# One more group of four w2 tiles in seven products in the third block, with its rows loaded and scaled there, and the middle blocks' order written out anew

## The chip, the cores and the metric

The kernel runs on one core of a Trainium2 chip. The metric is the device time of one execution in microseconds (us). A time of a kernel is the median of several executions; the profile is one further execution, with its own span.

## The reference

Only the part that matters for the computation is shown; A is a state-space layer, B a dense layer with a mish activation, and both work on the same normalised rows.

```python
xn = _layernorm(x, axis=-1)                      # x: 2048 rows of 1024
# A: a complex diagonal state per column, scanned over the rows
Lam_bar = jnp.exp(dt * Lam)
B_bar = ((Lam_bar - 1.0) / Lam)[:, None] * Bmat
Bu = jnp.einsum("bld,pd->blp", xn + 0j, B_bar)
for t in range(L):
    h = Lam_bar[None, :] * h + Bu[:, t, :]
y = 2.0 * jnp.einsum("blp,dp->bld", hseq, Cmat).real + xn * Dskip
# B: 1024 -> 3584 -> 1024
g = jnp.einsum("bsd,df->bsf", xn, w1) + b1
sp = jnp.log1p(jnp.exp(-jnp.abs(g))) + jnp.where(g > 0, g, 0)
act = g * jnp.tanh(sp)
return x + y + jnp.einsum("bsf,fd->bsd", act, w2)
```

## The kernel before

The 2048 rows go through in four blocks of 512. A block normalises its rows, makes the hidden activations (product with w1, then mish), projects the rows into the state, scans, and at the end adds up in PSUM the product of the activations with w2 ("dense 2") and the output projection of the state. The first block (0 to 150 us) also prepares weights. In the second block the state projections are done in seven products instead of eight (sums of weight quarters against sums of row halves, Strassen's scheme), which costs VectorE, ScalarE and PSUM banks the work of putting the results together. The third and fourth block (`SPLIT`) also do the product with w1 that way, in seven "quads" of four tiles (letters p, q, s, w, x, y, z of `w_product` and `w_evacuate`; letters a to d are the state's `product` and `evacuate`), and most of dense 2.

**Dense 2 in the third block.** w2 has 28 tiles of 128 rows. A group g of four tiles (2g, 2g+1, 14+2g, 15+2g) can be done in seven products (`fast`, L1542) or as four plain tiles (`dense`, L1502). In the third block four groups go the fast way and twelve tiles plainly, in the fourth all seven groups:

```python
NFG = {2: 4, 3: GF}
PLAIN = [(f, f + 1) for f in (24, 10, 8, 22, 12, 26)]
PASSING = {8: 4, 22: 4}
```

The seven products run first (order `KIND`, L1209): of each product a TensorE matmul of 512 columns per tile pair and bank, then the plain tiles, eight matmuls a tile, then the state's projection. For a fast group its raw w2 rows are loaded (letter m, `d2_load`, on GpSimd's DMA queue), scaled row by row (letter h, `d2_row`, L1233, on ScalarE), and put into seven 256 KB units of a DRAM scratch `w2d`: three of them as they are, four as differences made by VectorE (`d2_sums`, L1252); each goes out as a GpSimd store (`d2_store`, L1230). A letter k in the order pops one pending sum with its store. The fifth group (tiles 8, 9, 22, 23) is plain in the third block, and its rows pass through the weight ring there as plain tiles; on that occasion ScalarE scales them into two free activation buffers (`PASSING`, `SCALED_AT`), and its sums and stores follow, so that the fourth block finds it in `w2d`.

**The ring.** All streamed weights go through seven slots of 512 KB (`ring`). SP issues the loads in a fixed order of items (`ring_load`, L426): "ws" (two 256 KB units of w1 quads, L455), "tp" (two units of `w2d`, L450), "w2" and "c" (a plain pair of tiles, a state row, L458). A load is issued when TensorE has finished with the slot's former item (`item_done`, L852), and it stands in SP's queue behind whatever was written there earlier. The stores of the second block's output (`O0`, L1692) go through SP as well.

**The order.** What stands around what is written by hand in two strings, `STEPS` for the third block and `LAST` for the fourth. Letters besides those above: r rotates a state column by its phase (`rotate_in`, L914 to L918 on VectorE: one operation of 2048 elements and two of 512), G scales an activation tile, g is mish, t makes the sums of activations for products 5, 6 and 7 (`act_sums`, L1363), u and I the first products of dense 2 and the evacuation of their banks ("kept", L1580), E the statistics of four 128-row tiles of the next block (`ln_stats_only`, L564 and L566), l loads the next block's x (four 256 KB loads on GpSimd, L398).

Of the kernel before, what the change touches and what calls it, by code (L numbers as in the profile page):

```python
# [9 lines left out]
P = 128  # L10
# [153 lines left out]
def build_kernel(nc, A_x, A_Lambda_re, A_Lambda_im, A_B_re, A_B_im, A_C_re, A_C_im,  # L164
# [43 lines left out]
    UNITS = [(REAL[QUADS.index(o[0])], int(o[1])) for o in STEPS.split() if o[0] in QUADS]  # L208
# [203 lines left out]
    items = []  # L412
    for blk in range(NB):
# [9 lines left out]
        items += [("c", j) for j in range(NJ)] if blk >= FAST else []  # L423
    n_loaded = [0]
# [573 lines left out]
    def w_product(blk, i, n):  # L998
# [28 lines left out]
        if not direct and half == len(units) - 1:  # L1027
            item_done()
# [160 lines left out]
    steps, later, held = [], [], []  # L1189
# [21 lines left out]
    D2_RAW += [(("a", 24), ("a", 10)), (("h", 0), ("h", 4)), (("h", 8), ("h", 12))]  # L1211
# [21 lines left out]
    def d2_row(n, slot=None):  # L1233
# [89 lines left out]
    CHUNKS = {2: ((0, 8),), 3: ((0, 6), (6, 12), (12, 14))}  # L1323
# [171 lines left out]
    def tail(blk, base):  # L1495
        near = blk < NB - 1
        first = [True] * 8

        def acc(u, lhsT, rhs, reads, last=False, tell=False, chained=False):
            st_ = first[u]  # L1500
            first[u] = False
            PE.mm(lambda e: e.matmul(ps[:, u, :], lhsT=lhsT, rhs=rhs, start=st_, stop=last, skip_group_check=blk in SPLIT),  # L1502
# [39 lines left out]
        def fast(n, i, k):  # L1542
# [9 lines left out]
            if n not in (1, 2, 3):  # L1552
                rhs = rhs.bitcast(f16)
# [486 lines left out]
```

## Time and profile before

| what | before |
|---|---|
| median of 3 runs | 587.75 us (587.65 to 588.03) |
| span of the profiled execution | 586.3 us |
| bytes moved by the DMA engines | 162.15 MB, mean 277 GB/s |

Stages of the third and fourth block, from the table of stretches (busy time of each engine; DMA is the mean busy share of the 16 DMA engines; the granted TensorE clock is 1.00 in every row):

| us | what runs | TensorE | VectorE | ScalarE | DMA | GB/s |
|---|---|---|---|---|---|---|
| 306.8 to 347.0 | block 3: quads p, q, s and state products a, b | 40.20 | 33.31 | 27.54 | 0.96 | 325 |
| 347.0 to 374.0 | products c, d, quads w to z | 26.95 | 24.35 | 22.29 | 0.99 | 349 |
| 374.0 to 391.5 | seven products of w2 and the last of quad z | 17.45 | 11.80 | 11.01 | 0.77 | 271 |
| 391.5 to 412.3 | twelve plain tiles | 20.70 | 20.59 | 18.57 | 0.86 | 245 |
| 412.3 to 446.9 | the state's projection, outputs | 34.44 | 34.19 | 6.89 | 0.64 | 221 |
| 446.9 to 487.0 | block 4: as the first row | 40.10 | 27.70 | 32.84 | 0.77 | 270 |
| 487.0 to 513.3 | as the second row | 26.29 | 21.64 | 23.12 | 0.89 | 319 |
| 513.3 to 586.3 | seven products of w2 for all groups, projection, outputs | 70.50 | 63.99 | 26.54 | 0.64 | 224 |

How to read it: a stage in which TensorE's busy time equals the length of the stretch is set by TensorE; where the DMA share is near 1 the DMA engines have nothing left. Busy time of matmuls is that of a pipeline, so the pace of one matmul is read from a group's busy time over its count. In the rows of the views, "out<-in" are the program's tile names, xN is a count, and "[0.52 <-ACT act L901]" behind an instruction is the idle time ahead of it on its engine and what ended it. In a table of waits the columns are time, count and longest; in the stretches, for each engine busy time and count, then granted clock, DMA share and GB/s.

### The profile page before, as it was taken

The page shows a single profiled execution, that of the slowest core. Times are in us where ns is not written, and L with a number is a line of the kernel's source. Part 1 is how long each engine was busy: PE and PEld are TensorE (multiplying, and loading weights), DVE is VectorE, ACT ScalarE, POOL GpSimd, SP SyncE. Part 2 cuts the span into 40 slices and gives each one's busy share as a digit, 9 for nine tenths or more (in the row PEclk, how much of TensorE's full clock was granted, in tenths as well). Part 3 has the DMA queues.
Part 4 walks back from the last instruction along what each step waited for, and adds up shares of the span by engine and source line. Part 5 has one row for each costly group of instructions (what it writes and reads, how often), then busy time and mean ns, then how long its engine had stood idle before and what let it go on. Part 6 is the DMA issues. An engine that isn't in the chain of part 4 may idle for free.

```text
span 586.3 us, 9768 instructions
## 1 busy us (share of the span) xinstructions
PE 581.0 (99%) x3599; PEld 353.9 (60%) x3635; DVE 513.4 (88%) x789; ACT 401.8 (69%) x541; POOL 150.7 (26%) x213
## 2 busy tenths in 40 slices
PE   9999999999999999999999999999999999999998
PEld 8644444444447887444448888644446888844444
DVE  6998999998997878999877889779999669789995
ACT  4859994658578868999916687959223798992330
POOL 2899300123524420441351241001010113100000
PEclk9999999999999999999999999999999999999999
DMA  9999998999688978999999899798865966998832
GB/s 244 306 243 247 245 186 202 316 301 360 185 303 287 357 249 293 316 321 255 345 375 345 305 309 382 257 344 209 306 210 191 346 237 241 326 324 318 293 113 73
DMA packets 116345, 162.15 MB, mean 277 GB/s; under 512 B 55882, under 2 KB 66762, under 8 KB 116298
## 3 DMA queue, kind: packets, MB, share of 16 engines
q1 hardware_dynamic: 99776, 109.67, 62.0%
q0 software_dynamic: 13440, 44.57, 21.7%
q10 hardware_dynamic: 3082, 7.29, 3.3%
q8 instruction: 29, 0.48, 0.3%
q14 instruction: 18, 0.15, 0.1%
HBM read 115.36 MB, written 34.08 MB: 255 GB/s over the span
## 4 chain that ended last, share of the span: by engine, by line
PE 93%; DVE 2%; ACT 2%; DMA 1%; issue 1%; POOL 0%; ACTq 0%; POOLq 0%
PE ps L1502 34%; PE ps L1024 19%; PE ps L948 13%; PE ps L1563 10%; PE ps L871 10%; PE ps L1438 5%; DMA act<-in_A_B_im_dram 1%; PE ps L680 1%; PE ps L689 1%; PE ps L642 1%; ACT act L894 1%; PE ps L1525 1%; ACT act L901 1%; DVE CT L835 0%; DVE CT L833 0%
## 5 line engine op out<-in xcount | busy, mean ns | idle before, releaser
L1502 PE MATMUL ps<-ring,act 128*128 128x512 bf16 x532 | 117.3, 379 | 0.6
L1502 PEld LDWEIGHTS ps<-ring,act 128*128 128x128 bf16 x544 | 53.2, 98 | 63.8
L1044 ACT ACTIVATE snaps<-ps,par,cs 128x256 f32<-128x256 f32 x100 | 54.4, 562 | 44.4 <-PE ps L1024 40.0
L1502 PE MATMUL ps<-ring,hT 128*128 128x512 bf16 x355 | 78.3, 379 | 0.4
L1024 PE MATMUL ps<-TT,ring 128*128 128x256 f16 x552 | 68.3, 273 | 0.0
L910 DVE TENSOR_TENSOR mt<-hT,tab 128x2048 bf16<-128x2048 bf16 (+1 forms) x56 | 67.9, 1213 | 0.4
L1502 PEld LDWEIGHTS ps<-ring,hT 128*128 128x128 bf16 x362 | 35.4, 98 | 42.7
L1453 DVE TENSOR_TENSOR_SCAN hT<-cs,qi,hT 128x512 bf16<-128x512 f32 x48 | 60.7, 1275 | 0.0
L1024 PEld LDWEIGHTS ps<-TT,ring 128*128 128x128 f16 (+1 forms) x552 | 53.8, 98 | 7.2 <-issue 0.2
L871 PE MATMUL ps<-xnT,ring 128*128 128x512 bf16 x258 | 56.8, 379 | 0.3
L1024 PE MATMUL ps<-xnT,ring 128*128 128x256 bf16 x424 | 53.9, 273 | 0.0
L1061 DVE SCALAR_TENSOR_TENSOR act<-ps,cs,snaps 128x512 bf16<-128x512 f32 x54 | 39.8, 748 | 15.2 <-PE ps L1024 13.3
L1024 PEld LDWEIGHTS ps<-xnT,ring 128*128 128x128 bf16 (+1 forms) x424 | 41.4, 98 | 5.4
L871 PEld LDWEIGHTS ps<-xnT,ring 128*128 128x128 bf16 x264 | 25.8, 98 | 30.9
L1230 POOL DMA_DIRECT2D w2d<-act x21 | 15.0, 718 | 110.5 <-ACT act L1240 54.9
L1473 ACT ACTIVATE hT<-hT,wz 128x1024 bf16<-128x1024 bf16 x16 | 18.1, 1146 | 34.3 <-DVE hT L1468 34.3
L1563 PE MATMUL ps<-ring,act 128*128 128x512 bf16 (+1 forms) x176 | 39.5, 379 | 0.2
L1230 POOL DMA_DIRECT2D w2d<-hb x28 | 20.0, 717 | 74.4 <-ACT hb L1240 33.0
L894 ACT ACTIVATE act<-act 128x2048 bf16<-128x2048 bf16 (+3 forms) x13 | 33.0, 2557 | 3.8 <-DVE act L1047 3.8
L973 DVE TENSOR_TENSOR hT<-ps,snaps 128x512 f16<-128x512 f32 x36 | 23.8, 687 | 12.3 <-ACT snaps L965 11.1
L1563 PEld LDWEIGHTS ps<-ring,act 128*128 128x128 bf16 (+1 forms) x180 | 17.6, 98 | 20.6
L1173 POOL DMA_DIRECT2D wsd<-hb x35 | 19.1, 548 | 39.0 <-DVE hb L1199 28.8
(240 smaller groups left out, 1085.2 us busy)
## 6 DMA issues: line engine op xcount, KB each, us to landing
ring<-wsd SPq DMA_DIRECT2D x122, 256.0 KB, 4.6
ring<-in_B_w_dram SPq DMA_DIRECT2D x54, 512.0 KB, 5.9
ring<-ctd SPq DMA_DIRECT2D x24, 512.0 KB, 4.4
ring<-w2d SPq DMA_DIRECT2D x24, 512.0 KB, 4.6
wsd<-hb POOLq DMA_DIRECT2D x35, 256.0 KB, 5.1
ring<-w2d SPq DMA_DIRECT2D x29, 256.0 KB, 3.8
w2d<-hb POOLq DMA_DIRECT2D x28, 256.0 KB, 5.5
w2d<-act POOLq DMA_DIRECT2D x21, 256.0 KB, 6.2
```

The lines of the kernel that those rows point to most:

```text
L871: PE.mm(lambda e, k=k, w=w: e.matmul(ps[:, bank, :], lhsT=w, rhs=xnT[:, k, :], start=k == 0, stop=k == NK - 1), reads=[b_ring[s]] + b_xnT, ...
L894: aop(lambda e: e.activation(t, t, AF.Mish), reads=b, writes=b)
L910: vop(lambda e: e.tensor_tensor(mt[:], u.unsqueeze(1).to_broadcast([P, 2, 2, TB]), tab[:, :, j, :].unsqueeze(2).to_broadcast([P, 2, 2, TB] ...
L948: PE.mm(lambda e, w=w, x=x, o=o, begin=begin, end=end: e.matmul(ps[:, bank, o:o + TH], lhsT=w, rhs=x, start=opens and begin, stop=end, ski ...
L1024: PE.mm(lambda e, w=w, x=x, o=o, begin=begin, end=end: e.matmul(ps[:, bank, o:o + TH], lhsT=w, rhs=x, start=opens and begin, stop=end, ski ...
L1044: aop(lambda e, o=o, p=p, j=j: e.activation(o, p, AF.Identity, scale=ig, bias=b1(f0 + j)), reads=[b_ps[b], b_par, b_ig], writes=b_dst)
L1061: vop(lambda e: e.scalar_tensor_tensor(out=dst, in0=bank(b), scalar=ig, in1=src, op0=ALU.mult, op1=ALU.add), reads=[b_ps[b], b_snap[k], b_ ...
L1230: PO.dma(lambda e: e.dma_start(w2d[at // 4][:, at % 4 * TB:(at % 4 + 2) * TB].rearrange("p (j t) -> p j t", j=2), t[:, :, d, :]), sem, rea ...
L1438: PE.mm(lambda e, j=j, ci=ci, k=k, bank=bank: e.matmul(ps[:, bank + ci, :], lhsT=BT[:, ci, j, k, :], rhs=xnT[:, k, :], start=k == 0, stop= ...
L1453: vop(lambda e: e.tensor_tensor_scan(out=hT[:, ci, j, :], data0=cj("r", j).to_broadcast([P, TB]), data1=hT[:, ci, j, :], initial=init, op0 ...
L1502: PE.mm(lambda e: e.matmul(ps[:, u, :], lhsT=lhsT, rhs=rhs, start=st_, stop=last, skip_group_check=blk in SPLIT), reads=reads, writes=[b_p ...
L1563: PE.mm(lambda e: e.matmul(ps[:, bank, :], lhsT=lhsT, rhs=rhs, start=st_, stop=end, skip_group_check=True), reads=b_t + [b_ring[s]], write ...
```

## The change

The fifth group of w2 is done in seven products in the third block too (`NFG[2]` 5, eight plain tiles instead of twelve). Its rows do not pass through the ring: they are loaded raw by GpSimd (m4) in the third block into activation buffers 8 and 12 and scaled there by VectorE (H16 to H19, `d2_row` with `queue=VE`), and sums and seven stores follow. Each sum over the activations covers ten tiles a half instead of eight.

The two strings are written anew: evacuations are operations of their own (e and the product's name), and what stood in the functions `tail`, `dense_part` and `dense_fast` (products D and X, kept banks kp, plain tiles pl, scans sc, outputs Y, Q, fin, ...) stands in the strings as well, run by a new function `split_block`. Rotations r3 to r7 stand between the seven products. The stores of the second block's output (now o0) stand between the quads x and z, and the next block's x is loaded (l0) behind z6 and g2 where it stood behind h7. A ring slot is freed when the last matmul that reads it is written, whichever product that is in.

```diff
-    NFG = {2: 4, 3: GF}
+    NFG = {2: 5, 3: GF}
-    PLAIN = [(f, f + 1) for f in (24, 10, 8, 22, 12, 26)]
-    PASSING = {8: 4, 22: 4}
-    SCALED_AT = {24: (8, 22), 10: (12,), 8: (26,)}
+    PLAIN = [(f, f + 1) for f in (24, 10, 12, 26)]
+    PASSING = {}
...
-             "b5 O0 a6 b6 O0 a3 h4 b3 S0 O0 a7 O0 h5 b7 k0 c2 d2 k0 h6 a4 b4 h7 l0 k0 c5 c1 k0 d5 d1 r0 c6 G0 c3 G1 d6 d3 c7 G2 w1 d7 r1 w5 w2 G3 c4 d4 k0 E0 E1 w6 x1 x5 x2 k0 w7 k0 w3 r2 "
-             "x6 w4 k0 y1 y5 y2 x7 x3 E2 E3 y6 x4 z1 z5 g2 z2 y7 y3 z6 G7 y4 g6 z3 z7 u0 t0 G8 u2 G9 z4 I2 G10 u1 t1 t2")
...
+             "es6 m1 q4 eq4 k0 k0 a2 ea2 g0 a1 ea1 s7 es7 b2 eb2 k0 s3 es3 b1 eb1 s4 es4 a5 ea5 b5 g1 eb5 k0 a6 ea6 h4 a3 O0 b6 ea3 m4 eb6 O0 S0 O0 a7 ea7 "
+             "b3 ed2 eb3 b7 O0 eb7 h5 c2 ec2 k0 a4 k0 h6 d2 h7 b4 ea4 G1 eb4 d5 ed5 k0 k0 c1 ec1 c5 r0 c6 ec5 d1 ed1 H16 H17 ec6 G0 c3 w1 ec3 d6 ed6 H18 "
+             "c7 ec7 d3 H19 ed3 G2 ew1 d7 ed7 w5 ew5 G3 c4 ec4 k0 w2 k0 d4 ew2 k0 r1 ed4 w6 ew6 x1 ex1 k0 G4 x5 ex5 w7 ew7 k0 x2 ex2 o0 w3 ew3 r2 x6 w4 k0 "
+             "ex6 y1 ey1 o0 y5 ew4 k0 ey5 y2 ey2 o0 x7 ex7 x3 ex3 y6 ey6 x4 o0 ex4 z1 ez1 z5 ez5 z2 ez2 y7 ey7 y3 z6 k0 g2 l0 ey3 ez6 G7 y4 ey4 g6 z3 ez3 "
+             "t0 z7 ez7 r3 D10 D11 G9 G11 G8 G10 z4 E0 ez4 kp2 D70 t1 G6 D71 G5 E1 g7 D20 G12 t2 D21 X5 E2 r4 kp0 E3 lr0 G13 r5 li0 r6 kp1 ns2 ns0 tr0 ns3 "
+             "r7 X6 tr3 kp3 pl24 tr2 pl10 ns1 tr1 pl12 sc00 sc01 sc10 pl26 to0 so0 sc11 T0 to1 X3 sc21 so1 al0 sc20 sc30 al1 to2 sc31 X4 so2 sc40 to3 al2 "
...
-    D2_RAW += [(("a", 24), ("a", 10)), (("h", 0), ("h", 4)), (("h", 8), ("h", 12))]
+    D2_RAW += [(("h", 8), ("h", 12)), (("h", 0), ("h", 4)), (("h", 8), ("h", 12))]
...
-    def d2_row(n, slot=None):
+    def d2_row(n, slot=None, queue=AC):
...
-        aop(lambda e: e.activation(o, x, AF.Copy, scale=wg[:, r:r + 1]),
-            reads=b_x + [b_wg], writes=b_t[2 * j:2 * j + 2])
+        put = ((lambda e: e.activation(o, x, AF.Copy, scale=wg[:, r:r + 1])) if queue is AC else
+               (lambda e: e.tensor_scalar(o, x, wg[:, r:r + 1], None, op0=ALU.mult)))
+        queue.op(put, reads=b_x + [b_wg], writes=b_t[2 * j:2 * j + 2])
...
-    CHUNKS = {2: ((0, 8),), 3: ((0, 6), (6, 12), (12, 14))}
+    CHUNKS = {2: ((0, 10),), 3: ((0, 6), (6, 12), (12, 14))}
...
+    def used(i):
+        left[i] -= 1
+        if left[i] == 0:
+            gone.add(i)
+            return True
+        return False
+
+    def release():
+        while n_item[0] in gone:
+            item_done()
...
+    def split_block(blk):
...
+        def mm2(bank, lhsT, rhs, reads, at, last=False, opens=False, chained=False, lo=0, hi=TB, tell=False):
+            freed = at is not None and used(at)
+            PE.mm(lambda e: e.matmul(ps[:, bank, lo:hi], lhsT=lhsT, rhs=rhs, start=opens, stop=last, skip_group_check=True),
+                  reads=reads, writes=[b_ps[bank]], first=opens or chained, last=last, chained=chained, tell=tell or freed)
+            if freed:
+                release()
...
+        run = {"r": rotate_in, "G": lambda n: act_scale(blk, n), "g": lambda n: mish(blk, n), "k": lambda n: pop_step(),
+               "m": d2_load, "M": lambda n: d2_load(n, AC), "h": d2_row, "H": lambda n: d2_row(n, queue=VE),
...
+               "E": lambda n: ln_stats_only(blk + 1, n), "S": lambda n: row_scales(), "l": lambda n: load_next(),
+               "K": lambda n: carry_on(), "O": lambda n: held.pop(0)(SP), "o": lambda n: held_out.pop(0)(SP),
```

GpSimd's queue where the third block prepares w2, before (`hb` and `act` are activation buffers, `xx` the rows of x, L1225 raw loads, L1230 stores to `w2d`, L1173 stores to the scratch of w1):

```order
L1225 DMA hb<-in_B_w_dram 128x2x1024 x2
L1173 DMA wsd<-hb 128x1024 x4
L1230 DMA w2d<-act 128x2x512 x2
L1230 DMA w2d<-hb 128x2x512 x3
L398 DMA xx<-in_A_x_dram 128x1024 x4
L1230 DMA w2d<-act 128x2x512 x2
L1230 DMA w2d<-hb 128x2x512 x4
L1230 DMA w2d<-act 128x2x512 x7
```

and now (L1263, L1268, L1211 and L407 are the same operations):

```order
L1263 DMA hb<-in_B_w_dram 128x2x1024 x2
L1211 DMA wsd<-hb 128x1024 x4
L1263 DMA hb<-in_B_w_dram 128x2x1024 x2
L1268 DMA w2d<-act 128x2x512 x2
L1268 DMA w2d<-hb 128x2x512 x3
L1268 DMA w2d<-act 128x2x512 x2
L1268 DMA w2d<-hb 128x2x512 x11
L407 DMA xx<-in_A_x_dram 128x1024 x4
```

A second raw load stands ahead of the stores, the fifth group's seven stores (the last seven of the x11, from `act` before) follow those of the fourth group directly, and the loads of x stand behind all of them.

SP's queue from the third block's first ring loads to the first loads for dense 2, before (L455 ring loads of w1 units, L450 of w2 units, L1692 output stores of 256 KB):

```order
L455 DMA ring<-wsd 128x1024 x32
L1692 DMA out_dram<-xx 128x1024
L455 DMA ring<-wsd 128x1024 x2
L1692 DMA out_dram<-xx 128x1024 x3
L1173 DMA wsd<-act 128x1024 x4
L455 DMA ring<-wsd 128x1024 x15
L450 DMA ring<-w2d 128x1024 x20
```

and now (L465, L460 and L1601 are the same operations):

```order
L1211 DMA wsd<-act 128x1024 x4
L465 DMA ring<-wsd 128x1024 x8
L1601 DMA out_dram<-xx 128x1024
L465 DMA ring<-wsd 128x1024 x4
L1601 DMA out_dram<-xx 128x1024
L465 DMA ring<-wsd 128x1024 x2
L1601 DMA out_dram<-xx 128x1024
L465 DMA ring<-wsd 128x1024
L460 DMA ring<-w2d 128x1024 x2
L1601 DMA out_dram<-xx 128x1024
L460 DMA ring<-w2d 128x1024 x23
```

The four output stores moved behind the stores to `wsd` and stand one by one among the last loads of w1 units and the first of w2 units.

VectorE in the seven products of w2, from the second sum over the activations on, before (L1363 the sums, L910 to L918 a rotation, L1580 the kept banks):

```order
L1363 TENSOR_TENSOR act<-act 128x8x256 x2
L910 TENSOR_TENSOR mt<-hT_49,tab 128x2048
L916 TENSOR_TENSOR hT<-mt 128x512
L918 TENSOR_TENSOR hT<-mt 128x512
L1580 SCALAR_TENSOR_TENSOR KS<-ps,wz,xx 128x512 x4
L910 TENSOR_TENSOR mt<-hT_49,tab 128x2048
```

and now, from the last sum on (L947 to L955 a rotation, L1702 kept banks, L574 and L576 the statistics of x, L614 and L615 the inverse root):

```order
L1402 TENSOR_TENSOR act<-act 128x10x256
L574 BN_STATS stats<-xx 128x6 x2
L576 BN_AGGR mv<-stats 128x2
L947 TENSOR_TENSOR mt<-hT_49,tab 128x2048
L953 TENSOR_TENSOR hT<-mt 128x512
L955 TENSOR_TENSOR hT<-mt 128x512
L1702 SCALAR_TENSOR_TENSOR KS<-ps,wz,xx 128x512 x2
L574 BN_STATS stats<-xx 128x6 x2
L576 BN_AGGR mv<-stats 128x2
L947 TENSOR_TENSOR mt<-hT_49,tab 128x2048
L953 TENSOR_TENSOR hT<-mt 128x512
L955 TENSOR_TENSOR hT<-mt 128x512
```

Statistics and rotations now stand between the sums and the kept banks, and the kept banks come in two pairs; the second pair follows after the inverse root and one more rotation.

More of the change, by code (lines that the diff above doesn't have):

```diff
@@ L1026, in w_product @@
                     reads=b_unit + b_x, writes=[b_ps[bank]], first=begin, last=end, chained=not opens)
[L1027 to L1028 removed]
+        if not direct and used(at):
+            release()
     def w_evacuate(blk, i, n, keep):
@@ L1542, in fast @@
-        def fast(n, i, k):
-            bank = BANKS[n][i]
-            st_ = first[bank]
-            first[bank] = False
-            p, ng = KIND.index(n), 2 * NFG[blk]
-            at = p * ng + k
-            if near and p >= 5:
-                at += 4 * len(PLAIN) + -5 * ng % 4
-            s = (base + at // 4) % NRING
-            rhs = ring[:, s, at % 4 * TB:(at % 4 + 1) * TB]
-            if n not in (1, 2, 3):
-                rhs = rhs.bitcast(f16)
-            if n in (1, 2, 4):
-                t, b_t = place(blk, k + (n != 1) * NF // 2)
-                q = i if n == 4 else 2 + i
-                lhsT, b_t = t[:, q * P:(q + 1) * P], [b_t.parts[q // 2]]
-            else:
-                t, b_t = act_sum(blk, {5: 0, 6: 1, 7: 2, 3: 3}[n], k, k + 1)
-                t = t[:, 0, k % 2, :] if len(t.shape) == 4 else t[:, 0, :]
-                lhsT = t[:, i * P:(i + 1) * P]
-            begin, end = k == 0, k == ng - 1
-            PE.mm(lambda e: e.matmul(ps[:, bank, :], lhsT=lhsT, rhs=rhs, start=st_, stop=end, skip_group_check=True),
-                  reads=b_t + [b_ring[s]], writes=[b_ps[bank]], first=begin, last=end, chained=begin and not st_,
-                  tell=i == 1 and (at % 4 == 3 or at == NT - 1 or near and p == 4 and end))
@@ L1660, in tail @@
                 dense(f, (base + f // 2) % NRING, opens)
-        if blk in SPLIT:
-            if near:
-                yield from dense_part()
-            else:
-                dense_fast()
-        for f in range(0 if blk in SPLIT else NF):
+        for f in range(NF):
             s = (base + f // 2) % NRING
```

385 lines of the change are left out of this document (222 added, 163 removed), and 12 rows, old and new, of tables (LAST, STEPS).

## The prediction

> **What bounds the kernel now.** I read the page first (its engine line and its groups), then the table of waits for TensorE alone, then its timeline where the edited work lies.
>
> ```profile
> span 586.3 us, 9768 instructions
> PE 581.0 (99%) x3599; PEld 353.9 (60%) x3635; DVE 513.4 (88%) x789; ACT 401.8 (69%) x541; POOL 150.7 (26%) x213
> L1502 PE MATMUL ps<-ring,act 128*128 128x512 bf16 x532 | 117.3, 379 | 0.6
> L1502 PEld LDWEIGHTS ps<-ring,act 128*128 128x128 bf16 x544 | 53.2, 98 | 63.8
> PE ps L642 <- DVE filler L468: 1.0, 1, 1.0
> PE ps L680 <- ACT xr L527: 0.2, 1, 0.2
> ```
>
> TensorE is busy for 581.0 of 586.3 us. Its only waits in the table are the two at the start, 1.2 us together. From the third block's first product to the last matmul nothing holds it up, so this profile has no stall that a new order could remove: the change can gain what it takes off TensorE and no more, and it loses whatever it makes TensorE wait. The pace follows from the two group rows: 544 weight loads stand for 544 matmuls (12 records are missing from the matmul row), so one 512-column matmul takes 117.3/544 = 0.2156 us; the 379 ns are its length in the pipeline.
>
> ```profile
> 328.80 18.49 PE ps L948 x168
> 352.53 20.96 PE ps L1024 x192
> 373.54 3.40 PE L1563 MATMUL ps<-ring,act 128*128 128x512 bf16 x15
> 376.78 1.04 PE L1024 MATMUL ps<-TT,ring 128*128 128x256 f16 x8
> ...
> 382.83 8.80 PE L1563 MATMUL ps<-ring,act 128*128 128x512 bf16 x39
> ```
>
> The first two rows are of the chain of waits, the others of TensorE's timeline. Up to 328.80+18.49 = 347.3 us run products that take nothing from the ring; then come w1 products at 20.96/192 = 0.1092 us a 256-column matmul, and from 373.5 us the third block's seven products of w2 (before 16 tiles, now 20).
>
> **The change part by part.** *Matmuls.* A group of four tiles done plainly is 4 x 8 = 32 matmuls of 512 columns; in seven products it is 7 x 2 x 2 = 28. The fourth block and all other products keep their counts. So 4 x 0.2156 = 0.86 us leave TensorE's path.
>
> *Ring.* A 512 KB slot feeds 16 short matmuls (16 x 0.1092 = 1.75 us) or 8 long ones of the seven products (8 x 0.2156 = 1.72 us), but 16 long ones of a plain tile pair (3.45 us). Two plain slots go and 3.5 fast ones come: 0.9 MB more in 0.86 us less. During w1 products and seven products alike TensorE eats 0.524 MB/1.735 us = 302 GB/s from the ring. What the queue and the DMA engines have left is in these rows (waits of SP between 345 and 395 us, DMA issues between 345 and 376 us, then stretches of 5 us with DMA share and GB/s at the end):
>
> ```profile
> SPq L136 <- PE ps L1024: 22.2, 25, 4.6
> ring<-wsd SPq DMA_DIRECT2D x14, 256.0 KB, 4.9
> ring<-w2d SPq DMA_DIRECT2D x12, 256.0 KB, 3.8
> 326.47 0.42 SPq L1692 DMA_DIRECT2D out_dram<-xx  x1
> 336.97 1.68 SPq L1692 DMA_DIRECT2D out_dram<-xx  x3
> 351.00:356.00 5.00, 5.00 (x49) 4.49 (x47) 4.86 (x10) 4.78 (x10) 0.71 (x1) 1.00 0.98 357
> 356.00:361.00 5.00, 5.00 (x49) 4.47 (x47) 4.96 (x9) 2.93 (x7) 1.43 (x2) 1.00 1.02 379
> 361.00:366.00 5.00, 5.00 (x48) 4.50 (x46) 4.41 (x7) 3.11 (x7) 0.72 (x1) 1.00 1.03 394
> 366.00:371.00 5.00, 5.00 (x48) 4.48 (x47) 4.01 (x8) 4.90 (x7) 0.00 (x0) 1.00 0.98 350
> 371.00:376.00 5.00, 4.95 (x35) 3.32 (x35) 4.54 (x7) 4.97 (x5) 0.00 (x0) 1.00 0.87 267
> ```
>
> SP waits for TensorE to empty a slot, so a load is issued about 6 slots x 1.735 = 10.4 us before its use; with 0.42 us between the two halves and 4.9 us to landing 5.1 us are to spare. The DMA engines are full (share 0.98 to 1.03) from 351 to 371 us, and four GpSimd stores pass in that time:
>
> ```profile
> 341.96 2.20 POOL L398 DMA_DIRECT2D xx<-in_A_x_dram  x4
> 353.27 0.71 POOL L1230 DMA_DIRECT2D w2d<-hb  x1 [7.68 <-DVE hb L1261]
> 357.89 0.72 POOL L1230 DMA_DIRECT2D w2d<-hb  x1 [3.92 <-DVE hb L1261]
> 358.99 0.71 POOL L1230 DMA_DIRECT2D w2d<-hb  x1 [0.37 <-DVE hb L1261]
> 362.16 0.72 POOL L1230 DMA_DIRECT2D w2d<-hb  x1 [2.46 <-DVE hb L1261]
> ```
>
> The change puts three things into that same stretch. The fifth group's seven stores (7 x 0.262 = 1.84 MB) now follow its scaling, behind product d3. The four output stores of 256 KB (1.05 MB), at 326 and 337 us before, are now spread among the ring's loads on SP, so each also stands ahead of loads in that queue. The four loads of the next block's x, at 342 us before, now stand on GpSimd behind the last of those stores, some four products (3.5 us) ahead of the first seven-product, so from about 370 us; I count 1.5 of them, 0.39 MB, before the place that matters. The raw load of 1 MB comes before 347 us, where the ring is full and rests, and I price it at 0 (if it were late the VectorE scaling would wait, see the rivals).
>
> The place that matters is the third ring slot of the first seven-product. Its first pass runs all ten rows for one bank, so that slot is wanted 8 matmuls after the first and not 16: 1.7 us sooner, at 373.5 + 1.7 = 375.2 us, and the 5.1 us to spare become 3.4 us, or 3.4 x 302 = 1.03 MB. From 347.3 to 375.2 us are 28 us. Supply is the doubtful figure. I take the mean of the two rows with a share over 1.00, (379+394)/2 = 386 GB/s, since in those the engines and not TensorE set the rate. Then (386-302) x 28 = 2.35 MB are free, less the 1.05 MB of the four old stores, 1.30 MB; with the 1.03 MB, 2.33 MB. Wanted are 1.84+1.05+0.39 = 3.28 MB. Short by 0.95 MB, or 0.95/0.386 = 2.5 us that TensorE waits at the ring. Behind it the rest of x (0.66 MB) fits into 84 GB/s x 20 us, so the wait is not paid twice.
>
> Bounds: if most of the seven stores land before the ring begins to move, or loads and stores overlap better, the wait is 0. With the mean of all five rows, 349 GB/s, and all of x counted, (349-302) x 28 = 1.32, less 1.05, plus 1.03 = 1.30 MB against 3.93 MB: 2.63/0.349 = 7.5 us. I take 2.5 us.
>
> [...]
>
> *VectorE.* Four scalings go from ScalarE to VectorE, each sum over the activations covers 10 tile pairs instead of 8, and the statistics of x and three rotations now stand ahead of the evacuation that the plain tiles need (banks 5 and 7).
>
> ```profile
> L498 DVE TENSOR_SCALAR xn<-xx,mv,rs x2: 547/548/548, 10.8 to 12.8; 128x1024 bf16<-128x1024 bf16 x2
> 379.50 2.49 DVE L1363 TENSOR_TENSOR act<-act 128x2048 f16<-128x2048 bf16 x2 [0.52 <-ACT act L901]
> 354.44 1.37 DVE L564 BATCH_NORM_STATS2 stats<-xx 128x6 f32<-128x512 bf16 x2
> 355.85 0.21 DVE L566 BATCH_NORM_AGGREGATE mv<-stats 128x2 f32<-128x12 f32 x1
> L910 DVE TENSOR_TENSOR mt<-hT,tab 128x2048 bf16<-128x2048 f16 x5 | 6.1, 1222 | 0.1
> L916 DVE TENSOR_TENSOR hT<-mt 128x512 bf16<-128x512 bf16 x5 | 2.1, 425 | 0.2
> L1580 DVE SCALAR_TENSOR_TENSOR KS<-ps,wz,xx 128x512 f32<-128x512 f32 x4 | 2.8, 745 | 2.8 <-PE ps L1563 2.8
> ```
>
> The scaling is not in this trace; its nearest row is the 0.55 us of a tensor_scalar of one shape (half of that to 1.1 us as ends), so 2.2 us for four, among evacuations that wait for products anyway. Later: a sum is 1.23 x 10/8 = 1.53 us, a row's statistics 1.37+0.21 = 1.58, a rotation 1.22+2 x 0.42 = 2.07. From the second sum, which waits for ScalarE till about 379.5 us, to the first half of that evacuation: 2 x 1.53 + 3 x 1.58 + 3 x 2.07 + 3 x 0.745 + 0.33 for the root = 16.6 us, done at 396.1. Without a ring stall TensorE comes there after 20 + 8 short + 84 matmuls, 373.5+4.3+0.9+18.1 = 396.8. Before, VectorE stood idle there for 2.8 us; now 0.7 us are left, so I price this at 0 to 1 us when the ring is on time and at 0 when TensorE is 2.5 us late.
>
> **Sum.** -0.86 + 2.5 = +1.6 us on the profiled 586.3: 587.9. The median of the runs shown, 587.75, lies 1.45 above that span, so 589.4. The evacuations and rotations written out anew in the fourth block move no matmul, and its 2.2 us tail behind the last one is as before: 0.
>
> **The rivals.** *The gain arrives.* The ring's 5.1 us and stores that land in its rest swallow everything. For it: no ring load makes TensorE wait before. Against it: full engines for 20 us. 587.75-0.86 = 586.9, up to 587.9 with the VectorE term. *The x loads come late.* The first row's statistics stand on VectorE ahead of the evacuation of z4, which the second pass of the next product needs.
>
> ```profile
> xx<-in_A_x_dram POOLq DMA_DIRECT2D x12, 256.0 KB, 7.6
> ```
>
> Issued at 371 us and 7.6 us under way, x lands at 378.6; statistics and evacuation take 1.6+1.1 us, to 381.3, where TensorE arrives at 378.7+2.2 = 380.9. It decides from about 7.2 us to landing on; at 11 us the wait is 3.8 us, 590.7. *The wait is long and TensorE then runs slowly.* Rows of the chain:
>
> ```profile
> 4.16 1.71 PE ps L642 x16
> 9.68 2.73 PE ps L680 x24
> 12.41 0.45 PE ps L516 x8
> ```
>
> At the start 128-column matmuls take 0.107 us and soon afterwards 0.056. A wait near the upper bound could bring that half pace back: with a wait of 4 us and at most the 6 us up to the first fast stretch at half pace, 3 us more, 587.75-0.86+4+3 = 593.9. [...]
>
> **How the numbers follow.** A ring wait as forecast (about 1 to 5.5 us): 0.50, 589.4. The gain arrives, with or without the VectorE term: 0.35. Late x: 0.11. Half pace: 0.04. A measurement of this kernel tells about 0.2%, 1.2 us, from no change: that is 586.6 to 588.9. The full gain lies inside, so faster has only 0.04, for savings that the rows do not show; same gets the other 0.31 of the gain case and the forecast's waits under 2 us, 0.08, together 0.39; slower 0.57. The range 586.8 to 592.5 reaches from the full gain to a ring wait of 5.6 us and leaves out about 0.15; the forecast's own range is 588.0 to 592.5.
>
> **What would show it.** TensorE's row of waits would name ring loads near the start of the seven products of w2 in the third block, about 2.5 us in all; DMA share would stay at 1.0 from 350 to beyond 375 us; matmuls would be 4 fewer. If that row stays empty the ring term is wrong and the time is below 588. If TensorE waits there for VectorE, its evacuations and not the ring are the price; if it waits over 5 us, the supply is nearer 349 GB/s. Any stall outside the third block contradicts me.

## The result

| | before | changed |
|---|---|---|
| median | 587.65 us (587.32 to 588.03, 7 runs) | 591.34 us (589.88 to 596.88, 7 runs) |
| span of the profiled execution | 586.3 us | 589.9 us |

The changed kernel is slower: its time over that of before is 1.0075, with a 95% interval of 1.0056 to 1.0095. Its executions also spread over 7 us, those of before over 0.7 us.

TensorE's table of waits (waited for: time, count, longest) of the changed kernel now has two rows that were not there before, the first 2.5 us long:

```profile
PE ps L1644 <- DMA ring<-w2d: 2.5, 3, 1.6
PE ps L985 <- DVE hT L1010: 1.1, 1, 1.1
PE ps L654 <- DVE filler L478: 1.0, 1, 1.0
```

Its timeline (start, length, what; idle time ahead and its releaser in brackets) tells where they lie:

```profile
349.02 1.04 PE L1062 MATMUL ps<-TT,ring 128*128 128x256 f16 x8
351.12 1.05 PE L985 MATMUL ps<-TT,BT 128*128 128x256 f16 x8 [1.06 <-DVE hT L1010]
...
374.71 1.03 PE L1644 MATMUL ps<-ring,act 128*128 128x512 bf16 x4
376.20 1.04 PE L1644 MATMUL ps<-ring,act 128*128 128x512 bf16 x4 [0.46 <-DMA ring<-w2d]
378.88 2.76 PE L1644 MATMUL ps<-ring,act 128*128 128x512 bf16 x12 [1.64 <-DMA ring<-w2d]
...
384.23 3.20 PE L1644 MATMUL ps<-ring,S 128*128 128x512 f16 x14 [0.42 <-DMA ring<-w2d]
```

The first seven-product begins at 374.71; its second slot is late by 0.46 us, its third by 1.64, and one slot of product 7 by 0.42. The other wait, at 351 us, is for VectorE. The chain of waits shows what VectorE had been waiting for:

```profile
332.80 5.58 DMA wsd<-hb
...
338.95 0.70 POOL hb L1263
339.66 8.90 DMA hb<-in_B_w_dram
348.56 0.03 issue
348.58 0.04 DVE hb L1279
...
350.46 0.61 DVE hT L1010
351.07 0.05 issue
351.12 1.05 PE ps L985 x8
```

The load of the fifth group's raw rows waited for a store out of the same buffers (first row), was issued at 338.95, took 8.9 us to land, and VectorE stood at the first scaling until then, with evacuations behind it that TensorE needed.

The sum closes when starts are compared. From the third block's first w1 product to the fourth block's first it was 140.04 us before (306.68 to 446.72) and is 143.31 (306.98 to 450.29), 3.27 us more. Four matmuls less are -0.86. The late raw rows cost 351.12 - (349.02 + 0.87) = 1.23. The ring's three waits are 2.52 in the table and 2.52 + 3 x 0.163 = 3.01 by starts, because the modelled end of a matmul (0.379 us) lies 0.163 behind the next one's place (0.216). Together 3.38; 0.1 is not placed. The blocks ahead are 0.30 longer, the fourth block takes 139.6 us in both.

The DMA issues between 345 and 376 us (count, KB each, median us to landing), which before had w2 loads landing in 3.8 us:

```profile
ring<-w2d SPq DMA_DIRECT2D x12, 256.0 KB, 7.5
w2d<-hb POOLq DMA_DIRECT2D x11, 256.0 KB, 5.7
out_dram<-xx SPq DMA_DIRECT2D x4, 256.0 KB, 6.7
xx<-in_A_x_dram POOLq DMA_DIRECT2D x4, 256.0 KB, 7.6
```

and the stretches of 5 us (DMA share and GB/s at the end):

```profile
361.00:366.00 5.00, 5.00 (x49) 4.47 (x47) 4.69 (x8) 3.41 (x7) 1.43 (x2) 1.00 1.03 371
366.00:371.00 5.00, 5.00 (x49) 4.49 (x47) 1.26 (x3) 4.69 (x9) 0.00 (x0) 1.00 1.04 379
371.00:376.00 5.00, 4.73 (x40) 3.62 (x37) 4.89 (x9) 4.97 (x4) 2.88 (x5) 1.00 0.99 333
376.00:381.00 5.00, 3.16 (x14) 1.31 (x15) 4.33 (x7) 5.00 (x8) 0.00 (x0) 1.00 1.03 402
381.00:386.00 5.00, 4.58 (x26) 2.29 (x25) 4.01 (x7) 5.00 (x9) 0.00 (x0) 1.00 1.00 358
```

Before, the engines' share fell to 0.87 and 0.50 in the rows from 371 and 376 us; now it stays full to 386 us, and TensorE stands still in just those rows.

### The profile page after: what moved, and what is told of

Read it like the earlier page. It is cut to its first block, busy times and chain, and to the rows that moved or that the text cites. A ratio compares the mean times of both kernels' runs of the same rounds, so it can differ in the third digit from the quotient of the medians.

```text
span 589.9 us, 9783 instructions
## 1 busy us (share of the span) xinstructions
PE 582.8 (99%) x3631; PEld 353.2 (60%) x3631; DVE 513.4 (87%) x793; ACT 397.9 (67%) x537; POOL 151.9 (26%) x215
## 4 chain that ended last, share of the span: by engine, by line
PE 92%; DMA 5%; DVE 1%; SPq 1%; issue 0%; POOL 0%; DVEq 0%; POOLq 0%
PE ps L1540 26%; PE ps L1644 23%; PE ps L1062 18%; PE ps L908 10%; PE ps L985 9%; PE ps L1477 5%; DMA ring<-w2d 2%; DMA hb<-in_B_w_dram 2%; DMA ring<-in_B_w_dram 1%; PE ps L701 1%; DMA wsd<-hb 1%; PE ps L692 1%; DVE hT L1010 0%; DVE snaps L1000 0%; SPq L407 0%
## 5 line engine op out<-in xcount | busy, mean ns | idle before, releaser
L1540 PE MATMUL ps<-ring,act 128*128 128x512 bf16 x448 | 97.2, 379 | 0.0
L1540 PEld LDWEIGHTS ps<-ring,act 128*128 128x128 bf16 x448 | 43.8, 98 | 52.4
L947 DVE TENSOR_TENSOR mt<-hT,tab 128x2048 bf16<-128x2048 bf16 (+1 forms) x56 | 67.9, 1212 | 0.2
L1644 PE MATMUL ps<-ring,act 128*128 128x512 bf16 (+1 forms) x268 | 59.2, 379 | 2.1 <-DMA ring<-w2d 2.1
L1644 PE MATMUL ps<-ring,hT 128*128 128x512 bf16 (+1 forms) x262 | 55.6, 374 | 0.0
L1268 POOL DMA_DIRECT2D w2d<-hb x35 | 25.1, 718 | 98.6 <-ACT hb L1278 49.3
L1644 PEld LDWEIGHTS ps<-ring,act 128*128 128x128 bf16 (+1 forms) x268 | 26.1, 98 | 33.6 <-DMA ring<-w2d 3.1
L1644 PEld LDWEIGHTS ps<-ring,hT 128*128 128x128 bf16 x262 | 25.6, 98 | 29.8
L938 ACT ACTIVATE act<-act,cs 128x512 bf16<-128x512 bf16 x48 | 30.8, 710 | 0.1
L1263 POOL DMA_DIRECT2D hb<-in_B_w_dram x8 | 5.7, 721 | 93.9 <-DVE xx L1759 77.9
```

Source lines behind the costliest of these rows:

```text
L938: aop(lambda e, a=a, y=y: e.activation(a, a, AF.Copy, scale=y), reads=[b_a, b_y], writes=[b_a])
L947: vop(lambda e: e.tensor_tensor(mt[:], u.unsqueeze(1).to_broadcast([P, 2, 2, TB]), tab[:, :, j, :].unsqueeze(2).to_broadcast([P, 2, 2, TB] ...
L1644: PE.mm(lambda e: e.matmul(ps[:, bank, lo:hi], lhsT=lhsT, rhs=rhs, start=opens, stop=last, skip_group_check=True), reads=reads, writes=[b_ ...
```

## The experiments

The working theory after the result: (a) the DMA engines are crowded from 350 to 385 us, and the sum of stores, outputs and x makes the ring late; (b) the raw rows land late and hold VectorE. All runs (there is no E5 or E6) are set against the kernel before on the same chip (median 587.7 to 588.0 us). "Third block" is the length by starts as above, in the profiled execution; the waits are TensorE's there, of one execution each. In E1 and E8 to E11 the ring wait lies at another place than in the changed kernel, as E1 shows below.

| run | median us | ratio, 95% interval | third block | ring wait | other waits in it |
|---|---|---|---|---|---|
| before | 587.65 | | 140.04 | 0 | 0 |
| changed | 591.34 | 1.0056 to 1.0095 | 143.31 | 2.5 | 1.1 VectorE |
| E1 outputs early | 588.62 | 1.0003 to 1.0020 | 140.17 | 0.5 | 0.3 VectorE |
| E2 outputs on another queue | 591.89 | 1.0035 to 1.0080 | 145.31 | 5.1 | 0 |
| E3 statistics of x late | 594.36 | 1.0101 to 1.0127 | 146.87 | 1.8 | 3.5 ScalarE |
| E4 scaling late | 589.40 | 1.0026 to 1.0071 | 141.16 | 1.6 | 0 |
| E7 before, with the moves | 595.53 | 1.0117 to 1.0143 | 147.66 | 0.3 | 3.8 ScalarE |
| E8 outputs and x early | 592.58 | 1.0054 to 1.0099 | 144.77 | 0.9 | 2.4 VectorE |
| E9 as E8, scaling late | 591.99 | 1.0061 to 1.0085 | 145.14 | 0.6 | 3.2 VectorE |
| E10 as E9, sum early | 592.62 | 1.0072 to 1.0103 | 144.71 | 0.7 | 2.6 VectorE |
| E11 as E1, statistics behind z4 | 589.41 | 1.0019 to 1.0043 | 141.75 | 1.4 | 0.5 VectorE |
| E12 as E1, statistics and root late | 589.92 | 1.0021 to 1.0047 | 140.37 | 0 | 0.7 ScalarE |
| E13 statistics and root late | 590.60 | 1.0036 to 1.0087 | 143.57 | 2.3 | 0 |
| E14 the group's stores elsewhere | 590.29 | 1.0027 to 1.0059 | 140.33 | 0.3 | 0.5 VectorE |

**E1, E2: bytes or order of the queue.** E1 takes the four o0 between x2 and z1 out and puts them back to about their places of before:

```diff
-s7 es7 b2 eb2 k0 s3 es3 b1 eb1 s4 es4 a5
+s7 es7 o0 b2 eb2 k0 o0 s3 es3 b1 eb1 o0 s4 es4 o0 a5
```

E2 leaves them where they are and issues them from ScalarE:

```diff
-"o": lambda n: held_out.pop(0)(SP)
+"o": lambda n: held_out.pop(0)(AC if blk == 2 else SP)
```

> The changed kernel with its four output stores of 256 KB put back on SP before product b1 (some 20 us ahead of their places), all else the same. Bytes theory (full DMA engines make the ring late; 1.05 MB of output stores are part of a shortage of about 1 MB): TensorE's wait for ring loads in the seven products of w2 falls from 2.5 us to between 0 and 0.5 us, the wait for VectorE behind the late raw rows (1.1 us) stays, median about 588.4 us. Rival theory that x's loads alone, which land in the same 10 us, make the ring late: the ring wait stays above 1.5 us, median 590.5 us or more.

> The changed kernel with the four output stores at the same places of the order but issued on ScalarE's DMA queue. Bytes theory: the same bytes at the same time, ring wait 2 to 3 us, median 590.5 to 592 us. Queue rival (the stores hold up ring loads only by standing ahead of them in SP's queue, some 4 us of issue in all): ring wait under 0.7 us, median about 588.5 us.

TensorE's waits in E1:

```profile
PE ps L1644 <- DMA ring<-w2d: 0.5, 1, 0.5
PE ps L1644 <- DVE act L1085: 0.3, 1, 0.3
```

and in E2:

```profile
PE ps L1644 <- DMA ring<-w2d: 4.0, 3, 2.6
PE ps L1062 <- DMA ring<-wsd: 1.1, 1, 1.1
```

With 1.05 MB out of the stretch the median fell by 2.7 us, and the first slots of the seven products are on time. The 0.5 us that are left lie elsewhere, at a slot of product 2. Its chain in E1:

```profile
377.58 0.89 PE ps L1062 x8
...
379.85 5.58 DMA ring<-w2d
385.43 0.05 issue
385.48 0.60 PE ps L1644 x2
```

SP could issue that load, the third in a row, only after TensorE's product z4 (first row), and it landed 5.6 us later. In E8 to E11 the same slot is late by 0.6 to 1.4 us. In E8 the engines move only 134 GB/s from 381 to 386 us and 261 from 386 to 391, so full engines are not what makes this slot late.

In E2 the same bytes at about the same time (issued at 357.7 to 365.7 us, 358.0 to 369.4 in the changed kernel) on another queue left the ring as late or later (5.1 us). So it is the bytes that count and not the places in SP's queue. E1's profiled execution is its fastest; its others lie up to 2.3 us above, and what they wait for is not seen.

**E4: the raw rows.** The four scalings stand some 3 us later in VectorE's order.

```diff
-ed1 H16 H17 ec6 G0 c3 w1 ec3 d6 ed6 H18 c7 ec7 d3 H19 ed3 G2 ew1
+ed1 ec6 G0 c3 w1 ec3 d6 ed6 H16 H17 c7 ec7 d3 ed3 H18 G2 ew1 H19
```

> The changed kernel with VectorE's four scalings of the fifth group moved some 3 us later in VectorE's order (behind the evacuations of c3 and d6), so that VectorE does not stand at them when the raw rows land late. If those late rows cost TensorE the 1.1 us before 351 us: that wait goes, VectorE has no idle time ahead of the scalings, and the ring wait stays 2.5 to 3.3 us (stores no earlier), median about 590.3 us. Rival: the evacuations behind would be late anyway, the wait stays at 0.7 us or more, 591 us.

The wait at 351 us is gone, only the ring is left:

```profile
PE ps L1644 <- DMA ring<-w2d: 1.6, 3, 0.7
```

The median is 0.9 us below the 590.3 expected, and the ring wait too is shorter than expected. But in this execution the raw rows had landed early: the first scaling starts at 346.05, against 348.58 in the changed kernel, so E4 does not show that the move takes the wait away. How late the rows land differs between executions, and the wait for VectorE near 351 us goes with it. With the scalings where the change has them, the first one starts at 346.4 in E1, 347.0 in E2, 347.1 in E3 and 347.4 in E13, and TensorE does not wait; it starts at 347.8 in E8, 348.6 in E11, 349.0 in E14 and 348.6 in the changed kernel, and TensorE waits 0.3, 0.5, 0.5 and 1.1 us. E12 (348.9) has no such wait, but there TensorE had already stood 0.7 us at 343.4.

**E3, E13: x late in the order.** In the string the x loads go behind the second bank of product 7, the statistics behind the kept banks; E13 also has root and normalising behind the last kept bank. E3:

```diff
-z6 k0 g2 l0
+z6 k0 g2
...
-z4 E0 ez4 kp2 D70 t1 G6 D71 G5 E1 g7
+z4 ez4 kp2 D70 t1 G6 D71 l0 G5 g7
...
-X5 E2 r4 kp0 E3 lr0 G13 r5 li0 r6 kp1 ns2 ns0 tr0 ns3 r7 X6 tr3 kp3 pl24
+X5 r4 kp0 E0 G13 r5 E1 r6 kp1 E2 E3 lr0 li0 ns2 ns0 tr0 ns3 r7 X6 tr3 kp3 pl24
```

and E13 against E3:

```diff
-r6 kp1 E2 E3 lr0 li0 ns2 ns0 tr0 ns3 r7 X6 tr3 kp3 pl24
+r6 kp1 E2 E3 r7 X6 kp3 lr0 li0 ns2 ns0 tr0 ns3 tr3 pl24
```

> The changed kernel with the next block's x loads moved behind the second bank of product 7, and the four statistics behind the kept banks. Bytes theory as predicted (0.39 MB of x count before the place that matters, about 1 us): ring wait falls from 2.5 to about 1.5 us, median about 590.2 us. Rival that x is the main part: ring wait under 0.5 us, median about 588.6 us. Rival that x counts nothing: unchanged, 591.3 us.

> The run with x late again, with the root and the normalising behind the last kept bank on ScalarE, outputs at the places of the change. The 3.5 us wait for ScalarE and the lower clock behind it go; the ring wait stays 1.5 to 2 us (1.84 + 1.05 MB wanted, 2.33 MB free, 0.56 MB short); median 588.8 to 590 us. Rival: TensorE waits again, for another reason than the ring, and the time stays over 592 us.

E3's waits:

```profile
PE ps L1644 <- ACT KS L1708: 3.5, 1, 3.5
PE ps L1644 <- DMA ring<-w2d: 1.8, 2, 1.2
```

These two runs do not test late x loads. On GpSimd the loads still follow the same store of the fifth group, and they are issued as before. The changed kernel's first three loads, then E13's:

```profile
373.11 1.63 POOL L407 DMA_DIRECT2D xx<-in_A_x_dram  x3
371.94 1.63 POOL L407 DMA_DIRECT2D xx<-in_A_x_dram  x3
```

In E3 they go out at 371.58, in E12 at 373.42. Only the statistics, and in E12 and E13 the root and the normalising, came later. So the ring waits of 1.8 (E3) and 2.3 us (E13) against 2.5 are the difference between executions, and what x counts at the ring is not shown. E3's time missed for another reason: ScalarE stood 9.56 us at the root, waiting for the late statistics, with the last kept bank queued behind it. E13 has that wait no more. In both the granted clock fell after a wait, in E3 after the one for ScalarE (0.50 from 405 to 407 us). Stretches of 1 us of E13, in which the wait of 1.74 us ends at 377.88 (granted clock third from the end):

```profile
376.00:377.00 1.00, 0.14 (x1) 0.00 (x0) 1.00 (x2) 1.00 (x3) 0.00 (x0) 1.00 1.03 412
...
378.00:379.00 1.00, 1.00 (x3) 0.30 (x3) 0.23 (x1) 1.00 (x3) 0.00 (x0) 0.50 1.03 399
379.00:380.00 1.00, 1.00 (x4) 0.32 (x3) 0.00 (x0) 1.00 (x3) 0.00 (x0) 0.50 1.04 387
380.00:381.00 1.00, 1.00 (x4) 0.44 (x3) 0.00 (x0) 1.00 (x3) 0.00 (x0) 0.50 1.04 381
381.00:382.00 1.00, 1.00 (x6) 0.38 (x4) 0.00 (x0) 0.48 (x1) 0.00 (x0) 0.86 0.70 258
```

Twelve matmuls took 4.43 us there; after the 1.64 us wait of the changed kernel the same twelve took 2.76. The half clock cost 1.7 us.

**E7: the moves without the group.** The kernel before with outputs between quads x and z, x behind z6, statistics among the rotations.

```diff
-s7 O0 s3 O0 b2 b1 k0 O0 s4 g1 k0 O0 a5
+s7 s3 b2 b1 k0 s4 g1 k0 a5
...
-b4 h7 l0 k0
+b4 h7 k0
...
-k0 E0 E1 w6 x1 x5 x2 k0
+k0 w6 x1 x5 x2 o0 k0
...
-y1 y5 y2 x7 x3 E2 E3 y6 x4 z1
+y1 o0 y5 y2 o0 x7 x3 y6 x4 o0 z1
...
-z6 G7
+z6 l0 G7
...
                     for j in range(4, NJ):
+                        ln_stats_only(blk + 1, j - 4)
                         rotate_in(j)
```

> The kernel before (four fast groups, twelve plain tiles) with the moves of the change alone: its four output stores on SP spread between quads x and z, the next block's x loaded behind z6, the four statistics among the rotations behind the first kept banks. Bytes theory: 1.05 MB of outputs and 0.39 MB of x move into the stretch, 1.44 MB of the 2.3 MB that I had counted as free; no seven further stores; TensorE's ring wait 0 to 0.5 us, median 587.7 to 588.5 us. Rival that the moves and not the fifth group cost the time: ring wait 2 us or more, median 589.5 us or more.

```profile
PE ps L1504 <- ACT act L901: 3.8, 1, 3.8
...
PE ps L1565 <- DMA ring<-w2d: 0.3, 1, 0.3
```

On the ring the theory holds: the moves alone make it 0.3 us late, although the x loads, with none of the group's stores ahead of them, go out earlier than in the changed kernel (363.7 to 373.6 us). The time says nothing of it, because, as in E3, ScalarE stood at the root for late statistics (7.4 us idle), and here the activations of the plain tiles were queued behind it; half clock followed for 6 to 7 us (0.50 in each row of 1 us from 403 to 409 us). That is the price of where I put the statistics, not of the change.

**E8, E9, E10: everything early.** As E1, with x's loads back behind h7; E9 adds E4's order, E10 also pops the last sum of w1 units earlier. E8 against E1:

```diff
-d2 h7 b4
+d2 h7 l0 b4
...
-z6 k0 g2 l0
+z6 k0 g2
```

and E10 against E9:

```diff
-b1 eb1 o0 s4 es4 o0 a5 ea5 b5 g1 eb5 k0 a6
+b1 eb1 k0 o0 s4 es4 o0 a5 ea5 b5 g1 eb5 a6
```

> The changed kernel with the four output stores and the next block's x loads at their places of before, so that of the three additions only the fifth group's seven stores (1.84 MB) are left in the stretch. Bytes theory: 1.84 MB of 2.3 MB free, ring wait 0 to 0.5 us, what remains is the raw rows' chance of being late (0 to 1.1 us), median 587.0 to 587.9 us. Rival that the stores by themselves make the ring late: ring wait over 1 us, 588.5 us or more.

> As the run before (outputs and x early), with VectorE's four scalings some 3 us later in its order too. If nothing but the two causes named (crowded DMA engines, late raw rows) stands against the gain of four matmuls, TensorE has no wait left in the third block: median 586.9 us, below the kernel before. Rival that the later scalings push the last stores into the first w2 loads: ring wait of 0.5 to 1.5 us, 587.5 to 588.5 us.

> As the run before, and the last pending sum of w1 units before the raw load (whose store the load waits for) popped some 3 us earlier, behind b1. The raw load goes out about 3 us sooner, the fifth group's stores may follow sooner: 586.8 to 587.2 us. Rival: the sum now stands ahead of evacuations that TensorE needs and costs 0.3 us or more in waits for VectorE before 335 us.

All three missed by about 5 us. In E10 the raw load went out 0.7 us sooner than in E9, not 3. E8's waits from 340 to 400 us on VectorE and TensorE:

```profile
DVE hb L1300 <- DMA w2d<-hb: 3.3, 2, 2.4
...
PE ps L1062 <- DVE act L1099: 2.1, 1, 2.1
...
PE ps L1644 <- DMA ring<-w2d: 0.9, 1, 0.9
```

The x loads now stand on GpSimd ahead of the group's stores. Between 340 and 380 us such a store took 7.2 us to land (median; 6.0 in the change). The sums overwrite in place what the three direct stores are still reading, so VectorE waits for those stores, and evacuations behind it come late. The DMA engines are as full as before, from 346 to 366 us at 398 to 407 GB/s and a share of 1.02 to 1.04; the first w2 slots are on time (the 0.9 us are those of product 2), and VectorE waits in their place. In E9 and E10 TensorE waits for the same evacuations, 3.2 and 2.4 us. In E8 too the clock was at 0.50, from 364 to 367 us.

**E11, E12: what is left of E1.** E12 is E13's order with E1's outputs (its x loads go out as in E1, see E13); E11 puts the first row's statistics behind z4:

```diff
-z4 E0 ez4 kp2 D70 t1 G6
+z4 ez4 kp2 D70 t1 E0 G6
```

> As the run with the outputs alone early (588.62 us), with the first row's statistics of x one place later on VectorE, behind the evacuation of z4 and the second sum, so that x landing late cannot hold up z4. If x landing late is part of what that run still lost (0.3 us in its profile, more in its slower executions): median 587.5 to 588.2 us and no wait for VectorE's evacuation of z4. Rival that only the ring is left: no change, 588.4 us or more.

> Outputs early and the next block's x behind the second bank of product 7, its statistics behind the kept banks, and now the root and the normalising behind the last kept bank on ScalarE too. Only the fifth group's stores are then added to the stretch, with nothing ahead of them on GpSimd's queue. Theory (crowded DMA engines; whoever is last in the crowd waits): ring wait 0 to 0.3 us, no wait of VectorE for stores over 1 us, median 586.9 to 587.6 us. Rival: VectorE, full from 391 to 447 us, cannot take the statistics that late and TensorE waits for scans or the next block's rows: 588.5 us or more.

In E11 the wait for z4 is gone, but the ring slot of product 2 was 1.4 us late and the median did not fall. In E12 the ring has no row at all. TensorE's waits:

```profile
PE ps L1062 <- issue: 0.9, 1, 0.9
PE ps L985 <- ACT snaps L1002: 0.7, 1, 0.7
```

From its first w2 product to the fourth block E12 took 72.61 us against 73.18 before: most of the 0.86 us appeared. It was given back: the 0.9 us are in the fourth block (140.8 us to the end instead of 139.6). VectorE's timeline there:

```profile
446.08 2.47 DVE L1759 SCALAR_TENSOR_TENSOR xx<-ps,wz,KS 128x1024 bf16<-128x1024 f32 x2
448.58 2.36 DVE L1767 TENSOR_TENSOR KS<-KS,xx 128x1024 f32<-128x1024 f32 x2
451.05 2.48 DVE L1759 SCALAR_TENSOR_TENSOR xx<-ps,wz,KS 128x1024 bf16<-128x1024 f32 x2
```

The last outputs left their banks at 453.5, 5.7 us after the fourth block's first product (447.85); before it was 4.2 us (450.9 against 446.72). The profile gives no releaser for the 0.9 us; that it is these banks is read from the times only.

**E14: without the group's stores.** The change's own order, with the seven stores of group 4 left out and seven of the same size written in the second block.

```diff
     def d2_store(g, n, h, d, sem):
+        if g == 4:
+            return
...
     def d2_load(g, queue=PO):
+        if g == 0:
+            for n in range(1, 8):
+                at = KIND.index(n) * NF // 2 + 8
+                PO.dma(lambda e, at=at: e.dma_start(w2d[at // 4][:, at % 4 * TB:(at % 4 + 2) * TB],
+                                                    BT[:, 0, 0, :, :].rearrange("p k t -> p (k t)")),
```

> The changed kernel in its own order, without the fifth group's seven stores in the stretch: its raw load, scalings and sums stay, the results are not stored; seven stores of the same 256 KB go out some 150 us earlier with other numbers, so that the later loads have something to read (the output is not the reference's). Left in the stretch of the three additions: outputs 1.05 MB and x 0.39 MB, 1.44 MB of the 2.33 MB counted as free. Theory that the sum of the bytes decides: ring wait 0 to 0.5 us, the rows of the third block after its first w2 product in 72.3 to 73 us, median 587.0 to 588.2 us (0 to 1.2 us of it for late raw rows). Rival that outputs and x late are enough without the stores: ring wait over 1.5 us, 589.5 us or more.

```profile
PE ps L985 <- DVE hT L1010: 0.5, 1, 0.5
PE ps L1549 <- DMA ring<-in_B_w_dram: 0.5, 1, 0.5
PE ps L1653 <- DMA ring<-w2d: 0.3, 1, 0.3
```

The ring wait fell to 0.3 us and the third block to 140.33, as the sum of bytes has it. Without the group's stores ahead of them the x loads went out earlier too, one by one from 364.6 to 374.5 us, each when an output store had landed. The median missed, 590.29. A small part of that is the displaced stores, a ring wait of 0.5 us at 231 us; the profiled execution is itself 1.2 us faster than the median, and what the slower ones wait for is not seen.

No version beats the kernel before; E1 comes nearest, 0.12% above it.

## Why the prediction was right, and where it was off

*Matmuls, -0.86 us.* Right in kind: E12 shows 0.57 us of it with the ring on time. It never reached the end of the kernel.

*Ring, +2.5 us at the third slot of the first seven-product.* Right in place: the largest part of the wait is at that slot. The runs show the cause. Where the outputs (E1, E8 to E12) or the group's stores (E7, E14) are out of the stretch, the slots of the first seven-product are late by 0 to 0.3 us; where both are in it (the changed kernel, E2, E3, E4, E13), on either queue, by 0.9 to 3.7 us. That spread also says that the size, 2.5 us in the table of one execution and 3.0 by starts, was met in part by luck. Two errors of the sum nearly cancel. From 347.3 to 375.2 us the engines moved 362 GB/s at a share of 1.00, not 386, which is 0.67 MB less over 28 us. And TensorE did not draw 302 GB/s from 347.3 on: w1 products stand without a break only from 352.5, and of the 48 matmuls before that 24 were the state's and took nothing from the ring, 0.79 MB less. The 362 GB/s were no ceiling either: in the rows of 5 us from 346 to 376 us, where the changed kernel moved 361 in the mean, E1 moved 388.5 and E12 387.3. Of x, all four loads were issued ahead of the late slot (373.1 to 375.7), not 1.5 of them, but the first was usable only at 380.0; how much x counts stays open.

*Raw load, 0.* This is the step that failed: "comes before 347 us, where the ring is full and rests, and I price it at 0". The load waits on GpSimd for a store from the same buffers to land and goes out only at 338.95; it lands at 348.56, and 1.23 us of TensorE's time went with it in the profiled execution (0 to 0.5 in those of E1, E2, E3, E8, E11 and E13). I had named what would then wait, and had not priced it.

*VectorE before the kept banks, 0 to 1 us.* No wait there in the changed kernel, as forecast. E12, with the statistics put late, loses 0.9 us behind the block's end, where VectorE's last outputs come late; that VectorE would bound the change's own order next is not shown.

*Late x.* Not in the changed kernel; 0.3 us in E1, where VectorE's evacuation of z4 stood behind the first statistics.

*Half pace.* I asked for a wait near the upper bound, about 4 us; that length was my estimate, and no run shows that it takes so much. The runs show half pace after waits of 3.5 (E3) and 3.8 us (E7), and already after one of 1.74 (E13). Three of the changed kernel's seven executions have a mean granted clock of 0.991 to 0.997 and took 592.5 to 596.9 us; the four at 1.000 took 589.9 to 591.3. So half pace goes with the slow end of the spread, though none of those three was profiled.

*The signs.* The row of ring loads, the DMA share near 1.0 to beyond 375 us (0.91 from 351 to 356) and four matmuls fewer (3631 weight loads instead of 3635) are there, and behind the start no stall lies outside the third block. The wait for VectorE at 351 us is not among the signs named.

The numbers: forecast +1.6 us on the span, measured +3.6. The 2.0 us between are 1.23 for the raw rows, 0.5 for the ring by starts (3.0 instead of 2.5), 0.3 ahead of the third block. 591.34 lies in the range of 586.8 to 592.5, with a term of 1.23 us in it that the sum did not have.

## What to carry to other kernels

Four matmuls were worth 0.86 us, and the 1.84 MB of stores that paid for them went into a stretch whose DMA engines had nothing left (a share of 0.99 to 1.04 from 356 to 386 us in the changed kernel): before a product is made cheaper, count the bytes of its preparation against the free bandwidth of the stretch they fall in, together with all else that is moved there. Moving a transfer within a stretch of full DMA engines chose who waits (the ring for 2.5 us in the changed kernel, or in E8 VectorE for 3.3 behind a buffer still being stored); moving it out of the stretch took the wait away at the first slots (E1, with 0.5 us left elsewhere). An order written down is not yet a time: in E3, E12 and E13 the x loads did not move, which only the timeline of their queue told. Give a load's wait for its buffer a price of its own, by the store that frees it and its own time to landing.

## What had not been expected of the hardware

TensorE's granted clock went to 0.50 after waits that were short: 1.74 us in E13 (with one of 0.53 shortly ahead) and 2.1 us in E8, while a wait of 1.64 us in the changed kernel left it at 1.00, and after one of 2.6 us in E2 TensorE kept its full pace (twelve matmuls in 2.76 us). Stretches of 1 us of E8, in which the wait ends at 363.03 (TensorE's busy time first behind the length, granted clock third from the end):

```profile
361.00:362.00 1.00, 0.00 (x0) 0.00 (x0) 1.00 (x2) 0.00 (x0) 0.00 (x0) 1.00 1.03 399
362.00:363.00 1.00, 0.00 (x0) 0.00 (x0) 1.00 (x3) 0.56 (x1) 0.72 (x1) 1.00 1.08 416
363.00:364.00 1.00, 0.97 (x7) 0.81 (x8) 1.00 (x1) 0.99 (x2) 0.00 (x0) 0.79 1.01 383
364.00:365.00 1.00, 1.00 (x7) 0.73 (x5) 0.97 (x4) 0.97 (x3) 0.00 (x0) 0.50 1.03 397
365.00:366.00 1.00, 1.00 (x7) 0.69 (x6) 0.97 (x2) 0.65 (x2) 0.00 (x0) 0.50 1.07 412
366.00:367.00 1.00, 1.00 (x6) 0.70 (x5) 0.94 (x2) 0.00 (x0) 1.00 (x2) 0.51 1.04 412
367.00:368.00 1.00, 1.00 (x12) 0.90 (x10) 0.47 (x1) 0.00 (x0) 0.43 (x1) 1.00 0.84 287
```

Where a row's clock lies between 0.50 and 1.00, its mean tells how much of the row was at half: here 0.42 of the row from 363 us, so 3.4 us in all. By the same sum it stayed at half for about 3.4 us in E13, E3, E9 and E10 and for 6.8 us in E7. The length of a single wait does not tell whether the clock falls: it fell after 1.74 us in E13 and did not after 2.6 us in E2. What decides is not shown by these runs.

The DMA engines moved 398 to 407 GB/s in each of the four rows of 5 us from 346 to 366 us in E8, above the 386 GB/s that the prediction took as the supply of full engines.
